# A planner's due times set anew in a gated-linear-attention and squared-ReLU kernel on one core

## The chip, the core and the metric

The kernel runs on one core of a Trainium2 chip. A core has five engines with a queue of instructions each: TensorE (PE, the matmuls; its weight loads are shown as PEld), VectorE (DVE), ScalarE (ACT), GpSimd (POOL) and SyncE (SP), which here issues all the DMAs. Every engine takes its own queue strictly in order; engines meet at semaphores only. The metric is the device time of one execution in microseconds. Three executions of the kernel before took 517.08, 519.09 and 520.18 us; the median is 519.09 us.

## The reference

```python
def _attn_ref(q, k, v, alpha):              # (4, 8, 768, 48) each
    state = np.zeros((B, H, D, D))
    for t in range(S):
        state = alpha[:, :, t, :, None] * state + np.einsum('bhd,bhe->bhde', k[:, :, t], v[:, :, t])
        y[:, :, t] = np.einsum('bhd,bhde->bhe', q[:, :, t], state)
    return y

def _moe_ref(x, w_in, w_out):               # (3072, 384), (384, 2048), (2048, 384)
    h = np.maximum(x @ w_in, 0.0)
    return h * h @ w_out
```

The attention's output, turned to (3072, 384), is the x of the second function. The weights arrive as float64, the rest as float32.

## The kernel before

**Blocks and groups.** The attention is computed in 24 blocks of 128 time steps (6 chunks of each of 4 batch entries; a block has all 8 heads). Two blocks make a pair, four blocks a group of 512 tokens: groups 0 to 5. While TensorE runs the feed-forward layers of group g, the attention of the two pairs of group g+1 is woven in between its matmuls. The first group's attention stands ahead of everything, in an order written out by hand (the string `first`, L980 to L989).

**Attention of a pair** (`attention`, L1018, with the step list `PLAN`, L996). Each step has an offset in units from the pair's start. `ln` (ACT) takes the logarithm of alpha; `sp` (DVE, L279, L280) splits it in two; `cs` (PE, L291, L292) sums it along time; `eb` and `ei` (ACT, L305, L310) make the decays; `mk` and `mq` (DVE, L314) scale k and q; `turn` (PE, L529) transposes them into four PSUM banks; `kc` and `qc` (ACT, L537) copy them out, eight copies for a pair. `ga` (L486) makes the scores and the state sums of the pair's first block in two banks (`sckv`) and begins the outputs y of the pair before in two more; `gb` (L509) ends y and does the scores and sums of the second block. Behind the scores DVE copies the masked part (`am`, L426), adds the state (`us`, L452, and `s`, L466) and multiplies it by the block's last decay row (`s`, L467). That row comes over DRAM: `bl` (SP, L327, `row<-b`) stores it, `br` (SP, L333, `last<-row`, two DMAs a block) loads it turned. Blocks 20 to 23 are the last chunk and need no state behind them. `ev` (L539, L562) copies y to x, twelve ACT copies for a pair, and frees the two banks.

**The feed-forward layers** (`layer_in`, L724, and `layer_out`, L884). From group 1 on the inputs and the weights are held as split values (a or b: the large part; l: the rest; d: a difference), so that a product takes three passes. The first layer has 16 h tiles of 128x512: `in_x(n)` is six matmuls, `in_y(n)`, two tiles later, three (L681). How an h tile is summed, put through ReLU and squared is told by a letter of a four-letter string, by n modulo 4 (`in_x`, `in_y`, `in_post`):

- D: ACT copies the tile out of PSUM (L696), DVE adds what `in_y` made (L594, which frees the bank), DVE does ReLU and square in one instruction (L710).
- A: ACT scales the tile in PSUM (L698), later takes ReLU out of PSUM (L715, which frees the bank) and squares (L719).
- M: as A, but DVE squares.

Then h is split as well: ACT makes the large part (L655), DVE the rest (L656) and the difference (L594). `split_h` keeps the parts in a ring of seven; `layer_out` puts split i no further ahead than seven tiles (`AHEAD + MORE`). In groups 2 to 4 the second layer is turned: `turned_x(n)` is six matmuls (L843), `turned_y` the d passes (L855). Groups 0 and 1 run part of the second layer as plain float32 (`out_plain`, L776, four PE instructions each), since the weights' parts are only just made there (`prepare`, L639: `cast_w` on ACT, `rest_w` and `diff_w` on DVE, and their stores).

**PSUM.** All eight banks are one pool: h tiles, `sckv`, y, T, cs and the sums of the second layer take them in turn.

**The streams.** The b parts stay in SBUF, the l and d parts are loaded again for each group from DRAM, 384 KB each (L648). `pump` (L644) issues the next load whenever a part was used up, as long as less than `room` parts are held; 16 of them are b parts, and the pool has 26 buffers.

**The planner.** `weave` (L1052) walks through the units of a group (`in_x` costs 1.05, `in_y` 0.53, `turned_x` 1.08, `out_plain` 1) and puts each event of the attention, of the weights' preparation and of the x splits (`splits_of_x`) ahead of the first unit that begins at or behind its due time. The due times are numbers in the table `AT` (L19): `g1` and `g` hold the starts of the pairs in group 1 and in groups 2 to 4, `ga` and `gb` their offsets, `gx` the x splits, `lead` the first h splits, `s0` and `ahead` how far the h splits run before the second layer, `w_first`, `w_in_at`, `w_in_by`, `wstep`, `o0`, `o2` the weights, `tp` and `tp1` the letters, `room1` and `room` the stream. Order matters only within an engine: what moves past work of other engines alone stands where it stood.

Of the kernel before, what the change touches and what calls it, by code (L numbers as in the profile page):

```python
# [15 lines left out]


GB = 4
AT = {'u0': 2, 'evs': 0.4, 'lead': 5, 'post': 3, 'w_first': (42.68, 45.29, 95.05), 'wstep': 2.32, 'w_in_at': 1.99, 'w_in_by': 3.14, 'room1': 24, 'room': 24, 's0': 1, 'ahead': 5, 'late': 23, 'xs': 0.22, 'g0': (-0.17, 20.59, 27.02), 'sc0': (2.36, 2.26, 2.42), 'g1': (4.41, 18.74, 27.21), 'g': (2.58, 19.59), 'g1x': 46.81, 'gx': 43.15, 'g0x': 55.58, 'k0': 2, 'h0': 20, 'k1': 5, 'h1': 0, 'h1by': 3, 'evs0': 0.13, 'tp': 'DAMD', 'tp1': 'AADD', 'split': 8, 'o0': (46.28, 49.2), 'o1': (), 'o2': (21.54, 19.65, 30.49, 25.39, 42.39, 50.96), 'str1': 13.05, 'ga': 10.14, 'gb': 12.14}  # L19


RUN = {0: 128, 32: 32, 64: 64, 96: 32}
# [3 lines left out]
def kernel(  # L26
# [243 lines left out]

    SPLIT = AT["split"]

# [314 lines left out]
    here, todo, room = {}, [], [22]  # L587
# [37 lines left out]
    def diff_w(w, p):  # L625
# [7 lines left out]
        for x in "ld":  # L633
            t = made.pop((x, w, p))
            if w == "i" or p >= NW - AT["k0"] or (x == "l" and p >= NW - AT["k1"]):
                here[x, w, p] = t
        pump()

    def prepare(at, w, p):  # L639
        step = AT["wstep"]  # L640
        fs = (cast_w, rest_w, diff_w)
        return [(at + i * step, f, (w, p)) for i, f in enumerate(fs)]
# [78 lines left out]
    def splits_of_x(at, g):  # L721
        return [(at + i * AT["xs"], f, (g, i % KM)) for i, f in enumerate((split_x,) * KM + (diff_x,) * KM)]

    def layer_in(g):  # L724
        units = []
        for n in range(NJ + 2):
            if n < NJ:
                units.append((1.05, in_x, (n,)))
            if 0 <= n - 2 < NJ:
                units.append((0.53, in_y, (n - 2,)))  # L730
            if 0 <= n - AT["post"] < NJ:
                units.append((0, in_post, (n - AT["post"],)))
            if AT["lead"] <= n < AT["lead"] + AHEAD and (g > 1 or AT["k1"] == NW):
# [240 lines left out]
    for x in "stky":  # L974
# [6 lines left out]
        zeros2 ln0 cs0 ln1 eb0 cs1 load0v ei0 mq0 mk0 load2a eb1 qT0 load3a qc0 mq1  # L981
        kT0 kc0 load1v ei1 qT1 mk1 load2k load2q qc1 sc0 kT1 weights0 kc1 kv0 load3q
        am0 lt1 sc1 ln2 us0 ln3 cs2 lt0 am1 load3k kv1 cs3 eb2 us1 ei2 gt1 mk2
        load2v ya0 weights1 yb0 lc1 gy0 eb3 kT2 mq2 load3v lc0 qT2 ei3 load4a zeros2
        st0 ea00 kc2 qc2 ed01 ed02 first0 zeros2 load4q mq3 zeros2 mk3 qT3 middle0
        qc3 kT3 second0 first1 kc3 lt3 lt2 sc2 kv2 am2 ea03 us2 sc3 kv3 gk3 middle1
        lc3 am3 us3 ha0 ya2 yb2 weights2 second1 weights3 ea20 lc2 ed21 ha1 ha3 ed22
        ed23 weights4 first2 st2 middle2 ha2 hb0 load4v hb1 st3 st1 load4k
    """  # L989
    for word in first.split():  # L990
        f = max((x for x in steps if word.startswith(x)), key=len)
# [167 lines left out]
```

## Time and profile before

| | us |
|---|---|
| median of three executions | 519.09 |
| lowest, highest | 517.08, 520.18 |
| the profiled execution, whole | 517.32 |
| its span in the profile | 515.3 |

Busy time of the engines by stage, from the view of windows of the profiled execution (the stages are cut where the groups' first `in_x` begins):

| stage | from, to (us) | PE | DVE | ACT |
|---|---|---|---|---|
| attention of group 0 and start | 0 to 30 | 27.76 | 19.25 | 17.98 |
| group 0 | 30 to 124.6 | 94.60 | 83.42 | 73.23 |
| group 1 | 124.6 to 212.65 | 87.18 | 74.88 | 59.92 |
| group 2 | 212.65 to 291.4 | 78.75 | 56.36 | 45.46 |
| group 3 | 291.4 to 371 | 78.69 | 52.68 | 45.45 |
| group 4 | 371 to 445.6 | 74.60 | 46.09 | 41.06 |
| group 5 and the end | 445.6 to 515.3 | 65.96 | 36.62 | 26.70 |

The span runs from the first instruction to the last; the 2 us between span and whole execution lie around it. A row of a group view gives line, engine, operation, out<-in, shape and count, then busy microseconds, mean nanoseconds of one, the idle time just before and what ended it. Consecutive instructions on DVE and ACT overlap a little, so that an instruction of 0.69 us takes some 0.6 us of the queue.

### The profile page before, as it was taken

What the parts mean: (1) busy time and instruction counts of PE and PEld (TensorE: products, weight loads), DVE (VectorE), ACT (ScalarE), POOL (GpSimd) and SP (SyncE); (2) the same over time, 40 slices, a digit from 0 to 9 for tenths busy, and PEclk for the clock granted to TensorE, in tenths of its full rate; (3) what the DMA queues carried; (4) which work ended last, traced back from release to release, by engine and by line L of the source; (5) the groups of instructions that cost most, each with busy time, mean ns of one, the idle gap of its engine ahead of it and who ended that gap; (6) DMA issues with size and microseconds to landing.
All of it is one profiled execution on the core that took longest, in us unless ns stands there. A gap on an engine that the chain in (4) does not pass through costs nothing.

```text
span 515.3 us, 12727 instructions
## 1 busy us (share of the span) xinstructions
PE 507.5 (99%) x5166; PEld 403.9 (78%) x5166; DVE 369.3 (72%) x640; ACT 309.8 (60%) x643; POOL 6.0 (1%) x33
## 2 busy tenths in 40 slices
PE   8999999999999999999999999999999999999997
PEld 6884456669887679988888887888888888888996
DVE  3798799879979868875886476685466486364861
ACT  4789875577879567386944174955175755164620
POOL 4000000000000000000000000000000000000000
PEclk9999999999999999999999999999999999999999
DMA  9989767153877886898876588966576534589301
GB/s 172 229 249 278 216 170 230 28 187 137 289 204 218 204 186 164 301 309 220 241 166 210 150 221 222 277 183 193 164 215 238 197 114 150 154 273 402 152 1 62
DMA packets 144795, 102.73 MB, mean 199 GB/s; under 512 B 116561, under 2 KB 118241, under 8 KB 144737
## 3 DMA queue, kind: packets, MB, share of 16 engines
q1 hardware_dynamic: 144736, 101.92, 69.0%
q8 instruction: 41, 0.67, 0.6%
q14 instruction: 18, 0.14, 0.1%
HBM read 84.57 MB, written 17.33 MB: 198 GB/s over the span
## 4 chain that ended last, share of the span: by engine, by line
PE 91%; DVE 4%; DMA 2%; SPq 1%; ACT 1%; issue 1%; DVEq 0%; POOLq 0%
PE h L681 29%; PE o L760 20%; PE o L843 13%; PE h L931 8%; PE o L855 6%; PE y L398 4%; PE sckv L418 2%; PE T L529 2%; PE sckv L441 2%; DMA last<-row 1%; PE cs L288 1%; DMA a_in<-in_alpha_dram 1%; PE zeros L384 1%; SPq L333 1%; DVE wl L618 1%; SPq L122 1%
## 5 line engine op out<-in xcount | busy, mean ns | idle before, releaser
L681 PE MATMUL h<-xa,wb 128*128 128x512 f32 x240 | 68.5, 393 | 0.9 <-DVE hid L594 0.9
L681 PE MATMUL h<-xl,wl 128*128 128x512 f32 x240 | 67.6, 390 | 0.0
L681 PE MATMUL h<-xd,wd 128*128 128x512 f32 x240 | 66.6, 392 | 0.0
L562 ACT COPY x<-y 32x256 f32<-32x256 f32 (+1 forms) x137 | 49.2, 365 | 25.3 <-PE y L398 23.1
L696 ACT ACTIVATE hid<-h 128x512 f32<-128x512 f32 x40 | 23.7, 600 | 61.2 <-PE h L681 61.2
L594 DVE TENSOR_TENSOR hid<-h,hid 128x512 f32<-128x512 f32 x40 | 27.6, 689 | 36.5 <-PE h L681 34.3
L681 PEld LDWEIGHTS h<-xl,wl 128*128 128x128 f32 x240 | 45.0, 188 | 9.7
L681 PEld LDWEIGHTS h<-xa,wb 128*128 128x128 f32 x240 | 44.4, 188 | 10.2 <-DVE hid L594 1.0
L681 PEld LDWEIGHTS h<-xd,wd 128*128 128x128 f32 x240 | 44.6, 188 | 9.3
L760 PE MATMUL o<-w_out,hid 128*128 128x384 f32 x144 | 48.9, 492 | 0.0
L931 PE MATMUL h<-x,w_in 128*128 128x512 f32 (+1 forms) x120 | 43.0, 511 | 0.0
L760 PEld LDWEIGHTS o<-w_out,hid 128*128 128x128 f32 x144 | 26.7, 190 | 17.2
L698 ACT ACTIVATE h<-h 128x512 f32<-128x512 f32 x40 | 23.3, 581 | 24.8 <-PE h L681 22.7
L655 ACT ACTIVATE ha<-hid 128x512 fp32r<-128x512 f32 x42 | 26.2, 637 | 15.9 <-DVE hl L656 11.4
L931 PEld LDWEIGHTS h<-x,w_in 128*128 128x128 f32 x120 | 22.4, 190 | 16.9 <-issue 13.4
L855 PE MATMUL o<-hd,wd 128*128 128x512 f32 x144 | 33.4, 391 | 0.0
L855 PEld LDWEIGHTS o<-hd,wd 128*128 128x128 f32 x144 | 26.8, 188 | 6.1 <-ACT o L848 0.6
L656 DVE SCALAR_TENSOR_TENSOR hl<-ha,hid 128x512 fp32r<-128x512 f32 x42 | 28.9, 687 | 3.5 <-ACT ha L655 3.5
L656 DVE SCALAR_TENSOR_TENSOR hx<-hx,hid 128x512 fp32r<-128x512 f32 x36 | 24.7, 686 | 9.1 <-ACT hx L655 9.1
L594 DVE TENSOR_TENSOR hd<-ha,hl 128x512 fp32r<-128x512 f32 x42 | 29.1, 692 | 1.7
L843 PE MATMUL o<-hx,wb 128*128 128x512 f32 x72 | 28.7, 399 | 0.0
L843 PE MATMUL o<-ha,wb 128*128 128x512 f32 x72 | 28.3, 393 | 0.0
(131 smaller groups left out, 987.5 us busy)
## 6 DMA issues: line engine op xcount, KB each, us to landing
wd<-do SPq DMA_DIRECT2D x37, 384.0 KB
wl<-lo SPq DMA_DIRECT2D x34, 384.0 KB
wl<-li SPq DMA_DIRECT2D x32, 384.0 KB
wd<-di SPq DMA_DIRECT2D x32, 384.0 KB
raw<-in_moe_w_in_dram SPq DMA_DIRECT2D x8, 768.0 KB
raw<-in_moe_w_out_dram SPq DMA_DIRECT2D x8, 768.0 KB
v_in<-in_v_dram SPq DMA_DIRECT2D x24, 192.0 KB
a_in<-in_alpha_dram SPq DMA_DIRECT2D x22, 192.0 KB
```

Of the source, the lines that this page charges most:

```text
L398: ins = nc.tensor.matmul(out=ys[e][64 * half : 64 * half + D + G * e, m % 2, p // 2, t], lhsT=lhsT, rhs=rhs, start=(half, e) not in seen, ...
L562: copy(out=x[kk][to : to + m, t : t + 2], in_=blk[n]["y"][e][r : r + m, :, p // 2],)
L594: nc.vector.tensor_tensor(out=o, in0=x, in1=z, op=op)
L655: nc.scalar.activation(out=a, in_=x, func=AF.Copy, scale=NEAR * E)
L656: nc.vector.scalar_tensor_tensor(out=l, in0=a.bitcast(FP32), scalar=-1.0 / E, in1=x, op0=ALU.mult, op1=ALU.add)
L681: nc.tensor.matmul(out=acc["h", j], lhsT=here[w, "i", p][:, kk, jj * 128 : (jj + 1) * 128], rhs=x_parts[x][:, kk], start=start and kk == 0 ...
L696: nc.scalar.activation(out=hid[j], in_=x, func=AF.Copy, scale=E)
L698: nc.scalar.activation(out=x, in_=x, func=AF.Copy, scale=1.0 + E)
L760: nc.tensor.matmul(out=acc[t][:, 0:DM], lhsT=lhs[:, t * C : (t + 1) * C], rhs=rhs, start=start, stop=stop, skip_group_check=True,)
L843: nc.tensor.matmul(out=acc[c], lhsT=by_parts(here[w, "o", p], jj, c), rhs=x, start=n == 0 and w == "b", stop=n == NJ - 1 and w == "l", ski ...
L855: nc.tensor.matmul(out=acc[c], lhsT=by_parts(here["d", "o", p], n % 2, c), rhs=h_diff[n], start=False, stop=last and n == NJ - 1, skip_gro ...
L931: nc.tensor.matmul(out=ps, lhsT=w[:, kk, c0 : c0 + 128], rhs=xT[g][kk][:, cols], start=(kk == 0), stop=(kk == KM - 1),)
```

## The change

No instruction is added or taken away but for one letter; what changes is the order in each engine's queue. In the table: the second pair of groups 2 to 4 begins 4.17 units earlier (19.59 to 15.42) and the first 0.28; the first pair of group 1 begins 3.27 units later. `ga` comes 0.82 units earlier in a pair, `gb` 0.83 later. The letters of groups 2 to 5 go from D A M D to D D A D. The h splits begin a tile earlier in the first layer, three of them instead of one stand ahead of the second layer, and they run up to 12 instead of 5 tiles ahead (the ring of seven still holds). The x splits of groups 2 to 4 begin 3.29 units earlier. The stream may hold 26 parts instead of 24 (25 in group 1). In groups 0 and 1 the preparation of a few weights and three h splits change places. In the order written out for the start, `mq2` goes ahead of `lc1`, and `lc0` and three loads of weights change places with work of other engines.

```diff
-AT = {'u0': 2, 'evs': 0.4, 'lead': 5, 'post': 3, 'w_first': (42.68, 45.29, 95.05), 'wstep': 2.32, 'w_in_at': 1.99, 'w_in_by': 3.14, 'room1': 24, 'room': 24, 's0': 1, 'ahead': 5, 'late': 23, 'xs': 0.22, 'g0': (-0.17, 20.59, 27.02), 'sc0': (2.36, 2.26, 2.42), 'g1': (4.41, 18.74, 27.21), 'g': (2.58, 19.59), 'g1x': 46.81, 'gx': 43.15, 'g0x': 55.58, 'k0': 2, 'h0': 20, 'k1': 5, 'h1': 0, 'h1by': 3, 'evs0': 0.13, 'tp': 'DAMD', 'tp1': 'AADD', 'split': 8, 'o0': (46.28, 49.2), 'o1': (), 'o2': (21.54, 19.65, 30.49, 25.39, 42.39, 50.96), 'str1': 13.05, 'ga': 10.14, 'gb': 12.14}
+AT = {'u0': 2, 'evs': 0.4, 'lead': 4, 'post': 3, 'w_first': (45.82, 44.44, 94.99), 'wstep': 2.31, 'w_in_at': 1.92, 'w_in_by': 3.02, 'room1': 25, 'room': 26, 's0': 3, 'ahead': 12, 'late': 23, 'xs': 0.35, 'g0': (-0.17, 20.59, 27.02), 'sc0': (2.36, 2.26, 2.42), 'g1': (7.68, 18.74, 27.21), 'g': (2.3, 15.42), 'g1x': 47.42, 'gx': 39.86, 'g0x': 55.51, 'k0': 2, 'h0': 16, 'k1': 5, 'h1': 0, 'h1by': 5, 'evs0': 0.23, 'tp': 'DDAD', 'tp1': 'AADD', 'split': 8, 'o0': (42.39, 46.35), 'o1': (), 'o2': (21.54, 19.65, 30.49, 26.1, 43.38, 50.96), 'str1': 14.0, 'ga': 9.32, 'gb': 12.97}
...
-        load2v ya0 weights1 yb0 lc1 gy0 eb3 kT2 mq2 load3v lc0 qT2 ei3 load4a zeros2
+        load2v weights1 ya0 mq2 yb0 lc1 gy0 eb3 kT2 lc0 load3v qT2 ei3 load4a zeros2
...
-        lc3 am3 us3 ha0 ya2 yb2 weights2 second1 weights3 ea20 lc2 ed21 ha1 ha3 ed22
-        ed23 weights4 first2 st2 middle2 ha2 hb0 load4v hb1 st3 st1 load4k
+        weights2 lc3 am3 us3 ha0 ya2 yb2 second1 weights3 ea20 lc2 ed21 ha1 ha3
+        weights4 ed22 ed23 first2 st2 middle2 ha2 hb0 load4v hb1 st3 st1 load4k
```

## The prediction

> **What bounds it now.** The page first: how much of the span has TensorE busy, and at what clock.
>
> ```profile
> span 515.3 us, 12727 instructions
> ...
> PE 507.5 (99%) x5166; PEld 403.9 (78%) x5166; DVE 369.3 (72%) x640; ACT 309.8 (60%) x643; POOL 6.0 (1%) x33
> ...
> PEclk9999999999999999999999999999999999999999
> ```
>
> A busy matmul may still be a stalled one, so the chain of waits is asked for its pitch:
>
> ```profile
> 280.44 10.96 PE o L855 x48
> ...
> 371.02 6.81 PE h L681 x30
> ```
>
> That is 0.228 and 0.227 us a matmul, and every long piece of L681 and L855 in the chain has this pitch. An in_x is thus 1.37 us, an in_y 0.68; the planner's unit is 1.3 us. The change adds no matmul, so the time can fall only by the waits that TensorE still has, and the view of waits, TensorE alone, lists them:
>
> ```profile
> PE warm L244 <- POOL s L67: 1.1, 1, 1.1
> PE h L681 <- DVE hid L594: 0.9, 1, 0.9
> PE cs L291 <- DVE us L452: 0.9, 1, 0.9
> PE cs L288 <- ACT a_in L267: 0.6, 1, 0.6
> PE sckv L418 <- DVE ks L371: 0.2, 1, 0.2
> ```
>
> First, fourth and fifth belong to the start, which keeps its order on PE. The second and third, 1.8 us, are all there is to win in the groups. The timelines tell where they are from. DVE in group 3:
>
> ```profile
> 312.83 0.36 DVE L466 TENSOR_TENSOR s<-sckv,us 128x192 f32<-128x192 f32 x1
> 316.78 0.36 DVE L467 TENSOR_TENSOR s<-s,last 128x192 f32<-128x192 f32 x1 [3.59 <-DMA last<-row]
> 317.05 0.68 DVE L594 TENSOR_TENSOR hid<-h,hid 128x512 f32<-128x512 f32 x1
> ```
>
> DVE stood 3.59 us for the last row of block 18; the add queued behind it frees a PSUM bank, and in_x(10), at 317.79, waited for that. The row is late since SP's queue was:
>
> ```profile
> 301.94 1.72 SPq L122 DMA_DIRECT2D a_in<-in_alpha_dram  x2
> 303.76 3.98 SPq L327 DMA_DIRECT2D row<-b  x1
> ...
> 310.87 4.38 SPq L333 DMA_DIRECT2D last<-row  x4
> ```
>
> The third wait, at 174.2, is DVE's backlog in group 1: scores of block 10 were masked at 173.05, 2.7 us behind their sums, and cs of block 12 wanted their bank.
>
> **The change, part by part.** I list each queue's order before and after by the due times, and count instructions by the durations of their rows (in the queue, 0.6 us for a DVE or ACT instruction of 0.69 or 0.6).
>
> *Group 1, third wait.* Ahead of the masks of block 10 DVE no longer has split 7 (0.69 + 0.69) and a rest_w (1.2): 2.6 us less. But the first pair's DVE work begins 3.27 units (4.3 us) later, and DVE waits for its first add at 9 us into the group, so that some of the relief goes. Counted through, the masks come 2.5 us behind the sums, much as before; but cs of block 12 now stands two units behind ga, not one: 1.29 us more. The 0.87 us goes but for 0 to 0.3; I take **-0.8**.
>
> *Group 3, second wait.* ga moves ahead of in_y(6), by 0.68 us, and gb behind in_x(10), so that 4.1 us of matmuls (in_y, in_x, in_y, in_x) stand between them where 2.05 stood. Should the row land at the same time, DVE waits 4.3 us, but in_y(6) is now an A tile, which needs no add, and TensorE next lacks a bank at in_x(11), about 318.5, with the add of tile 7 due at 318.3. 0.91 becomes 0 to 0.3: **-0.8**.
>
> *New waits, group 1.* At turn of blocks 8 and 9 mq(9) is behind an add, a rest_w and a diff_w more than before: it ends 20.0 us into the group, and is wanted at 19.9 without stall (0.5 at most if each DVE instruction costs 5% more). Queued behind it on DVE is the preparation of parts 5 and 6, for which only ACT and stores wait. **+0.3**. At turn of blocks 12 and 13 gb stands two units ahead, not three. The twelve ACT copies that free y's banks take 4.36 us; they began 1.8 us behind gb before, since a cast_w was ahead of them, and can begin at 0.8 now. They end 5.2 us behind gb's start, and turn's second half wants the banks at 4.7 to 4.8: **+0.4** (0 to 0.5). Behind it on TensorE is all else.
>
> *Groups 2 and 3, second pair.* Between cs and turn there are now 4.1 us of matmuls (in_y, in_x twice) instead of 5.5. ACT's queue from one to the other end of in_x(10) to cs: two ln (0.8), ReLU and square of tile 6 (1.15), the scaling of tile 10 (0.55), twelve copies (4.6), two copies of D tiles (1.0): 8.1 us in 6.7 us, so eb begins 1.4 us behind cs. Then eb, ei, eb, ei at 0.39 each, and DVE: mk, a square, mq, mk, mq, 0.5 to 0.6 each. mq(21) ends 4.9 us behind the start of cs and turn wants it 5.5 behind: 0.6 us to spare. **0**, with up to 1.4 us a group if ACT comes later. turn to ga: 3.4 us of matmuls, eight ACT copies (2.3 us) end 1.5 us ahead: 0. In group 4 the second pair has no new blocks.
>
> *Group 2, last rows of block 16.* DVE is ready for it 7.5 us behind turn's start (1.15 + 3.4 + scores and sums 1.1 + masks and adds 1.8). In the same pair before, turn was at 254.05 and the last SP issue of the rows ended at 258.6; with 2 us to land (the 1.9 of the chain's `last<-row`) that is 6.5 us. 1 us to spare: **0**, at worst, if the 3.98 us hold of group 3 comes here, DVE is 3 us late, split 3 with it, and turned_x(3) waits 1.6.
>
> ```profile
> 246.21 1.27 SPq L122 DMA_DIRECT2D a_in<-in_alpha_dram  x2
> ...
> 249.35 0.26 SPq L327 DMA_DIRECT2D row<-b  x1
> ```
>
> These packets are the one place where a page speaks against the change. The Trainium skill, "DMA: Bandwidth & Descriptors", Specifications, has line rate only from 512 B a transfer; the page of the profile counts 116,561 of 144,795 packets below that, the alpha loads' among them. By that rule every `row<-b` behind two alpha loads would be held, and the moved pair would pay the 1.6 us; the trace shows 3.98 us in one place and 0.26 here, so the loads alone don't do it.
>
> *M to D.* Four tiles a group leave ACT a scaling and a ReLU (581 + 596 ns) and take a copy (600); DVE gets an add (689) beside the square (686). ACT -2.3 us, DVE +2.8 us a group. DVE is busy 52.7 of 79.6 us in group 3: hidden, **0**; without that cover 2.8 us a group. The add frees a bank a unit sooner than the ReLU did.
>
> *h splits.* DVE needs 1.22 us for each (hl, hd), TensorE 1.37 for each turned_x, and the splits start as early as before or earlier: 0. Past ring place 7 ACT waits for the turned_x before; queued there are copies of y, which nothing wants for 15 us. *x splits*: wanted 10 us later, 0. *Group 0*: TensorE's order is untouched, the four weight parts and the h splits trade places within 25 us in which DVE has gaps of 3 us in all; 0 (-0.3 to 0.3). *The start*: only mq2 passes lc1 on DVE, 0.16 us, and qT2 waits for neither: 0.
>
> *Room.* A load now goes into the buffer just used, so SP follows TensorE instead of running two parts ahead of the frees; the parts land two uses sooner. No wait of the trace is on a streamed part: 0 in this execution. In the others, which took up to 2.9 us more, I can't see what they waited for; late rows and parts are the likeliest, and both are eased.
>
> **Sum**: -0.8 - 0.8 + 0.3 + 0.4 = -0.9; the profiled 517.32 (a span of 515.3 and 2.0 around it, which stays) becomes 516.4. The median of the runs before is 1.8 us above the profiled one; if all of that stays, the median is 518.2, if none, 516.4. I let a tenth to a fifth stay: **516.6**.
>
> **The rivals.** *B, no new wait*: the turns fit, and both waits go: 517.32 - 1.8 = 515.5, with the start's small change 515.3. For it: the margins that I find negative are 0.1 and 0.4 us. *C, given back*: the waits reappear elsewhere as PSUM stays as full (y's banks are held 1.65 units longer); or half the diff is without effect, as `ahead` over 7 and the moved weight loads are: 519. *D, slower*: the second pair, moved into the first layer, doesn't fit. Its place is turn at 22 units of groups 2 and 3, its price 1.4 us each for ACT's backlog plus 1.6 us for block 16's row: 517.32 - 0.9 + 4.4 = 520.8, with the median's 1.8 us 522.6. It decides once ACT is 0.6 us later at cs than I count. For it: ACT is busy 9.56 of 10 us from 240 to 250 before. Against: D tiles relieve ACT just there.
>
> **Chances.** Forecast 0.45 (its own range 515.0 to 518.3), B 0.18, C 0.14, D 0.23. A measurement of this kernel tells about 0.5% from no change: below 516.5 is faster, above 521.7 slower. Forecast gives 0.25 faster and 0.20 same; B faster; C same; D 0.22 slower, 0.01 same. Faster 0.43, same 0.35, slower 0.22. Range 513.8 (below B by a start or end that shrinks) to 522.6.
>
> **What would show it.** In the profile after: no wait of in_x on L594 near 317 and none of cs on `us` in group 1; turns of group 1 late by 0.3 to 0.4 us; turn of the second pair in groups 2 and 3 without a wait on DVE q_in. ACT falls by some 9 us, DVE grows by 11. A wait at these turns above 1 us, or of L467 on `last<-row` in group 2, proves D; PE waits of the same sum at other lines prove C.

## The result and the profile after

| | before | after |
|---|---|---|
| median of 13 executions, us | 518.25 | 516.34 |
| lowest, highest | 517.08, 520.18 | 515.71, 517.53 |
| the profiled execution, whole | 517.32 | 516.64 |
| its span | 515.3 | 514.6 |

The ratio is 0.9964, with a 95% interval of 0.9953 to 0.9975: 1.9 us are gone in the median, and only 0.7 us in the two executions that were profiled. That difference is what most of the experiments are about. The page of the kernel after, its first lines and its chain:

```profile
span 514.6 us, 12773 instructions
...
PE 508.3 (99%) x5166; PEld 404.6 (79%) x5166; DVE 377.0 (73%) x656; ACT 302.3 (59%) x627; POOL 6.0 (1%) x33
...
PE 96%; DMA 2%; SPq 1%; DVE 1%; issue 0%; ACT 0%; DVEq 0%; POOLq 0%
```

ACT has lost 7.5 us and DVE gained 7.7, as the letters want it. The view of waits for TensorE in the kernel after:

```profile
PE warm L244 <- POOL s L67: 1.1, 1, 1.1
PE cs L288 <- ACT a_in L267: 0.5, 1, 0.5
PE sckv L418 <- DVE hid L594: 0.2, 1, 0.2
PE sckv L418 <- DVE ks L371: 0.2, 1, 0.2
```

Both waits of 0.9 us in the groups have gone, and one new wait has come: `sckv` on L594. From each group's first in_x to the next one's, before and after (the differences of the starts in the timeline):

| stage | before | after | difference |
|---|---|---|---|
| start and group 0 | 124.43 | 124.36 | -0.07 |
| group 1 | 88.06 | 87.75 | -0.31 |
| group 2 | 78.75 | 79.42 | +0.67 |
| group 3 | 79.62 | 78.65 | -0.97 |
| group 4, group 5 and the end | 144.40 | 144.39 | 0 |

Group 3 shows how its wait went. DVE and then PE in the timeline of the kernel after:

```profile
317.05 0.36 DVE L467 TENSOR_TENSOR s<-s,last 128x192 f32<-128x192 f32 x1 [4.24 <-DMA last<-row]
317.33 0.68 DVE L710 SCALAR_TENSOR_TENSOR hid<-hid 128x512 f32<-128x512 f32 x1
317.93 0.68 DVE L594 TENSOR_TENSOR hid<-h,hid 128x512 f32<-128x512 f32 x1
```

```profile
317.90 0.66 PE L441 MATMUL sckv<-v_in,k_in 64*64 64x48 f32 x32
318.49 0.97 PE L681 MATMUL h<-xd,wd 128*128 128x512 f32 x3
319.30 0.85 PE L681 MATMUL h<-xa,wb 128*128 128x512 f32 x3
```

DVE stands longer than before (4.24 us, 3.59 then), and TensorE no longer notices, since the add that it wants comes after more of its own matmuls. In group 2 the same lateness is now felt. DVE and PE there:

```profile
237.04 0.36 DVE L467 TENSOR_TENSOR s<-s,last 128x192 f32<-128x192 f32 x1 [3.61 <-DMA last<-row]
237.31 0.68 DVE L710 SCALAR_TENSOR_TENSOR hid<-hid 128x512 f32<-128x512 f32 x1
237.92 0.69 DVE L594 TENSOR_TENSOR hid<-h,hid 128x512 f32<-128x512 f32 x1
```

```profile
238.14 0.28 PE L418 MATMUL sckv<-qs,ks 48*64 48x64 f32 x2
238.66 0.63 PE L418 MATMUL sckv<-qs,ks 48*64 48x64 f32 x27 [0.24 <-DVE hid L594]
```

Here `gb`'s second bank is the one that the add of 237.92 frees, and TensorE stands from 238.20 to 238.66.

### The profile page after: what moved, and what is told of

Read it like the earlier page. It is cut to its first block, busy times and chain, and to the rows that moved or that the text cites. A ratio compares the mean times of both kernels' runs of the same rounds, so it can differ in the third digit from the quotient of the medians.

```text
span 514.6 us, 12773 instructions
## 1 busy us (share of the span) xinstructions
PE 508.3 (99%) x5166; PEld 404.6 (79%) x5166; DVE 377.0 (73%) x656; ACT 302.3 (59%) x627; POOL 6.0 (1%) x33
## 4 chain that ended last, share of the span: by engine, by line
PE 96%; DMA 2%; SPq 1%; DVE 1%; issue 0%; ACT 0%; DVEq 0%; POOLq 0%
PE h L681 31%; PE o L760 22%; PE o L843 13%; PE h L931 8%; PE o L855 6%; PE y L398 4%; PE sckv L418 3%; PE T L529 2%; PE sckv L441 2%; PE cs L288 1%; DMA a_in<-in_alpha_dram 1%; PE zeros L384 1%; DMA last<-row 1%; PE cs L291 1%; SPq L333 1%; PE cs L292 1%
## 5 line engine op out<-in xcount | busy, mean ns | idle before, releaser
L696 ACT ACTIVATE hid<-h 128x512 f32<-128x512 f32 x56 | 33.7, 601 | 88.4 <-PE h L681 86.7
L681 PE MATMUL h<-xd,wd 128*128 128x512 f32 x240 | 68.4, 398 | 0.0
L594 DVE TENSOR_TENSOR hid<-h,hid 128x512 f32<-128x512 f32 x56 | 38.5, 689 | 33.9 <-PE h L681 33.6
L710 DVE SCALAR_TENSOR_TENSOR hid<-hid 128x512 f32<-128x512 f32 x56 | 37.8, 684 | 0.0
L594 DVE TENSOR_TENSOR hd<-ha,hl 128x512 fp32r<-128x512 f32 x42 | 29.1, 692 | 1.9
L843 PE MATMUL o<-hx,wl 128*128 128x512 f32 x72 | 28.0, 389 | 0.0
```

Of the source, the lines that this page charges most:

```text
L594: nc.vector.tensor_tensor(out=o, in0=x, in1=z, op=op)
L681: nc.tensor.matmul(out=acc["h", j], lhsT=here[w, "i", p][:, kk, jj * 128 : (jj + 1) * 128], rhs=x_parts[x][:, kk], start=start and kk == 0 ...
L696: nc.scalar.activation(out=hid[j], in_=x, func=AF.Copy, scale=E)
L710: nc.vector.scalar_tensor_tensor(out=h, in0=h, scalar=0.0, in1=h, op0=ALU.max, op1=ALU.mult)
L843: nc.tensor.matmul(out=acc[c], lhsT=by_parts(here[w, "o", p], jj, c), rhs=x, start=n == 0 and w == "b", stop=n == NJ - 1 and w == "l", ski ...
```

## The experiments

All are compared with the kernel before, run beside them on the same chip (its medians there were 517.67 to 518.47). The kernel after was not run beside them. A difference to it is one of medians taken at different times, between which the kernel before alone moves by 0.8 us; where it is small, the difference by the two ratios to the kernel before is given as well. The first four each take one part of the change alone.

**e1_pairs**

```diff
- 'g': (2.58, 19.59), 'gx': 43.15, 'ga': 10.14, 'gb': 12.14
+ 'g': (2.3, 15.42), 'gx': 39.86, 'ga': 9.32, 'gb': 12.97
```

> The kernel before with four due times of the kernel after alone: g, ga, gb and gx, that is the pairs of groups 2 to 4, their scores and the x splits. Theory (DVE's wait for the late last decay row is what the kernel before loses in groups 2 and 3, more in other executions than in the profiled one, and the wider distance of ga and gb takes it up): most of the 1.9 us, median 1.0 to 1.6 below the kernel before; TensorE's wait of in_x on L594 in group 3 is gone. Rival 'stream': at most 0.5 below. Rival 'letters' (without the D tiles ACT is too late for the second pair): slower than before by 0.5 to 2.8, with a wait at the second pair's turn.

Measured: 519.13 us, ratio 1.0014 (1.0000 to 1.0029). Groups 2 and 3 took 78.81 and 78.63 us, so the wait on L594 is gone as the theory has it, and turn waits for nothing. But group 1 took 90.51, 2.45 more than before. The view of waits for PE, and PE's timeline there:

```profile
PE y L398 <- issue: 1.5, 2, 1.1
...
PE sckv L441 <- issue: 1.2, 1, 1.2
```

```profile
179.07 0.32 PE L441 MATMUL sckv<-v_in,k_in 64*64 64x48 f32 x8
180.63 0.56 PE L441 MATMUL sckv<-v_in,k_in 64*64 64x48 f32 x24 [1.24 <-issue]
```

TensorE stops in the middle of one loop of equal matmuls, for "issue", that is for nothing that the profile knows. No theory of mine had that. The view of DMA has a queue of kind "instruction", 41 packets of 16 KB. I numbered TensorE's records (matmuls, weight loads, waits) from the start of the program, and looked where such stops lie: every one follows record 192 of a run of 256 (counted from 0), and ends 1.3 to 1.6 us behind the landing of one of these 41 packets. From the records:

```
kernel      place us  packet landed  TensorE goes on  later by
e1_pairs    169.63    169.66         170.95           1.29
e1_pairs    179.17    179.16         180.63           1.47
e2          16.96     17.12          18.52            1.40
e2          317.90    317.33         318.72           1.39
after       169.93    168.87         170.29           1.42
```

So TensorE waits for its own instructions. 256 of them are 29 us of large matmuls (0.227 us for a matmul and its weight load) and under 2 us of the scores (0.45 us for 32 and 32). A packet that comes late costs nothing in the first case and its whole lateness in the second. This became the new theory, "supply".

**e2_first_groups**: `g1`, `g1x`, `g0x`, `w_first`, `wstep`, `w_in_at`, `w_in_by`, `o0`, `o2`, `h0`, `h1by`, `str1` of the kernel after in the kernel before.

> The kernel before with the due times of groups 0 and 1 of the kernel after alone: g1, g1x, g0x, the w_ entries, o0, o2, h0, h1by, str1. Theory: only the wait of cs on us in group 1 is at stake, 0.9 us in the profiled execution; ga and gb keep their old offsets, so that the masks of block 10 come as late as before and cs of block 12 stands one unit behind ga: 0 to 0.6 below the kernel before. Rival 'first groups' (the median's gain is from group 1, where weights and pairs compete for DVE): 1.2 to 1.9 below.

Measured: 519.94 us, 1.0039 (1.0021 to 1.0057); the executions spread from 518.2 to 522.9. Group 1 took 87.94 us, and cs waits for `us` no more; both theories fall on the total. The profiled execution lost 1.56 us at 16.96 and 0.82 at 317.90, both places of the table above, and both in stretches that this edit leaves alone. What makes the packets land later there in this kernel was not found.

**e3_letters**

```diff
- 'tp': 'DAMD'
+ 'tp': 'DDAD'
```

> The kernel before with the letters D D A D in place of D A M D alone (four tiles a group copied by ACT, added and squared by VectorE). Theory: hidden work moved from ACT to DVE, 0, within 0.4 of the kernel before; DVE longer by some 7.7 us of busy time, ACT shorter by 7.5. Rival 'VectorE is what the row wait delays, and more work on it makes it worse': 0.5 to 1.5 above. Rival 'ACT frees banks late, the letters carry the gain': 1 to 1.9 below.

Measured: 517.90 us, 0.9998 (0.9988 to 1.0008): the letters alone are worth nothing in the median, as the prediction had it. In the profiled execution one wait changes. DVE stands 3.44 us for the row of block 18, and `ga` and `gb` are where they were, but the built program gives in_x(10) of group 3 the bank of tile 6 in place of that of tile 7, and it waits 0.23 us on L715 instead of 0.9 on L594. Stops for instructions (1.14 us in all, below) hide that in the total.

**e4_room**

```diff
- 'room1': 24, 'room': 24
+ 'room1': 25, 'room': 26
```

> The kernel before with the stream's room alone (26 parts held instead of 24, 25 in group 1). Theory: no wait is on a streamed part; SP's order changes around the last rows: 0, within 0.5 of the kernel before. Rival 'stream' (the other executions of the kernel before wait for parts or for rows behind a pump that runs ahead): 1 to 1.9 below.

Measured: 521.69 us, 1.0067 (1.0054 to 1.0079). Both theories are wrong. The orders of PE, DVE, ACT and POOL are those of the kernel before, only SP's differs. The view of waits for PE, and three windows:

```profile
PE h L681 <- ACT x L562: 2.5, 1, 2.5
```

```profile
319.00:323.00 4.00, 1.50 (x7) 0.94 (x6) 2.86 (x6) 3.17 (x9) 0.00 (x0) 1.00 1.08 295
323.10:326.40 3.30, 3.30 (x9) 2.53 (x9) 0.00 (x0) 1.01 (x3) 0.00 (x0) 0.50 0.44 88
326.50:330.00 3.50, 3.50 (x17) 2.86 (x17) 0.77 (x2) 1.85 (x4) 0.00 (x0) 1.00 0.71 227
```

(After the window and its length come the busy times of PE, weight loads, DVE, ACT and POOL, then TensorE's granted clock, the DMA share and GB/s.) in_x(11) of group 3 waits 2.5 us for the copies of y. Which bank a tile gets is fixed when the program is built: in the kernel before this tile has the bank of an h tile 15 tiles back, here that of `y` five tiles back, which `gb` has only just finished. Another order of loads was enough to change the choice. And the wait costs more than itself: behind it the granted clock stands at 0.50 for 3.4 us, which is 1.7 us more. 2.5 + 1.7 is most of the 4.3 us by which group 3 is longer (83.95); besides, in_x(10) has the bank of tile 6 here too and waits 0.4 us on L715 in place of the 0.9 on L594.

The next four take the kernel after and put one thing into it, or one part back.

**e5_shift**

```diff
+        for i in range(28 if _ == 2 else 0):
+            e, p = i % 2, i // 2 % NP
+            rows = slice(64 * e, 64 * e + 64)
+            nc.tensor.matmul(
+                out=t[rows, p, G:64], lhsT=s_t[0][rows, p, :], rhs=s_t[0][rows, p, G:64],
+                start=True, stop=True, skip_group_check=True,
+            )
...
-        warm(0)
+        warm(_)
```

> The kernel after with 28 small matmuls on zeros (112 instructions of TensorE) added to the warm-up at the start; nothing behind them changes. Theory 'supply': TensorE's instructions arrive by DMA in packets of 256 (the DMA view shows 41 of 16 KB); in every trace so far each stall put down to issue in the scores lies 192 instructions past a multiple of 256 and ends 1.4 us behind the landing of such a packet. In the kernel after only few of these places lie in or right behind a burst of small matmuls. 112 instructions more put three of them there, near 233, 257 and 312 us: 2.7 to 5.1 us above the kernel after, 519.0 to 521.5, with waits of 0.5 to 2 us for issue at these three places. Rival 'the place does not matter' (the stalls are a matter of DMA load alone): only what the added matmuls take at the start, at most 1 us: 516.3 to 517.4.

Measured: 528.77 us in the median of five executions, ratio 1.0188 to the kernel before (1.0154 to 1.0223), 12.4 us above the kernel after. Nothing behind the start was touched, the banks neither. The stops came at 237.48 (1.59 us), 262.35 (1.89; TensorE goes on 1.36 us behind a landing there too, though the profile names DVE) and 319.79 (3.23). PE's timeline (line numbers are 8 higher here), and the DMA view of the 1.6 us in which the packet for the third landed:

```profile
319.35 0.66 PE L406 MATMUL y<-am,v_in 64*48 64x64 f32 x27
323.03 0.33 PE L406 MATMUL y<-am,v_in 64*48 64x64 f32 x4 [3.02 <-issue]
```

```profile
DMA packets 1325, 0.17 MB, mean 104 GB/s; under 512 B 1324, under 2 KB 1324, under 8 KB 1324
...
q8 instruction: 1, 0.02, 5.6%
```

The places were told in advance within 8 us (233, 257 and 312), and they came later by about what the start and the earlier stops had added; the rival is out. The size was not: a fourth stop of 2.04 us fell at 16.50, and behind it and behind the one of 3.23 the clock was halved for 3.41 us each. Groups by parts: the start and group 0 are 4.8 us longer, group 2 is 2.7, group 3 is 4.9. The packet landed among 1,324 small data packets.

**e6_old_distance**

```diff
- 'ga': 9.32, 'gb': 12.97
+ 'ga': 10.14, 'gb': 12.14
```

> The kernel after with ga and gb at the offsets of the kernel before (10.14 and 12.14). Theory (the distance of 4.1 us of matmuls between the two bursts of scores is what takes up the late row and the instruction supply): the wait of in_x on L594 in group 3 is back, and 0.8 to 2.0 us above the kernel after, 517.1 to 518.3. Rival 'letters and room carry it': within 0.4 of the kernel after.

Measured: 525.02 us, 1.0143 (1.0125 to 1.0161), far above what was expected. The view of waits for PE:

```profile
PE h L681 <- ACT x L562: 2.4, 1, 2.4
PE T L529 <- DVE k_in L314: 2.4, 1, 2.4
...
PE h L681 <- ACT hid L715: 0.5, 1, 0.5
PE h L681 <- DVE hid L594: 0.3, 1, 0.3
```

The wait on L594 in group 3 is not back: in_x(10) has been given the bank of tile 6, an A tile, and waits 0.5 us on L715; the 0.3 on L594 is in group 2 (242.67). The large waits are others: turn in group 1 waits for its scaled k, and in group 3 in_x(11) has got the bank of y five tiles back once more, as in e4_room. Behind each of the two the clock is at half for 3.4 us. The wide distance is thus needed by the rest of the table as it is built; the expected sum was wrong since it priced one wait, and neither the bank nor the late k.

**e7_old_letters**

```diff
- 'tp': 'DDAD'
+ 'tp': 'DAMD'
```

> The kernel after with the letters D A M D of the kernel before. Theory: ACT has 0.5 to 0.6 us more to do between cs and turn of the second pair, and my count left 0.6 us to spare: 0 to 0.5 us above the kernel after, 516.3 to 516.9, no wait of turn above 0.3. Rival D of the prediction (the second pair fits only if ACT is relieved): 1.4 to 2.8 above, with T waiting for q_in at the second turn of groups 2 and 3.

Measured: 516.76 us, 0.9981 (0.9970 to 0.9992); 0.4 above the kernel after by the medians, 0.9 by the ratios, and no turn waits. Rival D of the prediction falls.

**e8_old_room**

```diff
- 'room1': 25, 'room': 26
+ 'room1': 24, 'room': 24
```

> The kernel after with 24 parts of the stream held, as before. In the kernel before, 26 instead of 24 cost 3.5 us, since the built program then gave in_x of group 3 the bank of y. Theory: room itself is worth nothing, and only the banks that come with it count; here two h tiles swap the banks of an h tile and of y, far behind y's copies: within 0.5 of the kernel after. Rival 'room is worth 3.5 us the other way here' or 'the stream needs it': 1 us or more above the kernel after.

Measured: 516.89 us, 0.9987 (0.9977 to 0.9997); 0.55 above the kernel after by the medians, 1.2 by the ratios. The profiled execution has one stop more, 0.59 us at 390.61 in group 4, a place of the supply. It stands in the two other wide-distance kernels with 24 parts as well (0.61 in e1_pairs, 0.61 in e11) and in none with 26 parts. A stop of that size, from SP's order around one packet of instructions, would be most of the 0.55; that it is the whole of what room is worth here is not shown. In e4_room the same step cost 3.5 us the other way, by a bank.

Two experiments then went for the late rows. Both exchange the loads of a pair's two rows: DVE wants the first block's first, and the plan issues it second.

**e9_rows_first**, in the kernel after, and **e10_rows_first_before**, in the kernel before:

```diff
-        (6.5, "turn br1"),
-        (7.0, "kc0 qc0 kc1 qc1 br0"),
+        (6.5, "turn br0"),
+        (7.0, "kc0 qc0 kc1 qc1 br1"),
```

> The kernel after with the two loads of last<-row of a pair exchanged: the pair's first block, whose row DVE wants first, is issued first (br0 with turn, br1 half a unit later). All banks stay as they are. Theory: in group 2 DVE stands 3.61 us at L467 for the row of block 14, and the add behind it holds up gb by 0.45 us; the row's two issues come 1.0 us earlier, DVE stands some 2.6 us, and 0.3 to 0.5 us go: 515.8 to 516.1. Rival 'backlog' (all four small loads land together when the queue is drained): DVE still stands 3.4 us or more, within 0.2 of the kernel after.

> The kernel before with the same exchange of the two loads of rows, banks unchanged. Theory: DVE's 3.59 us at L467 in group 3 become some 2.6, in_x(10) finds its bank, and the second wait of the prediction goes: 0.8 to 1.0 us below the kernel before. If late rows are also what the other executions of the kernel before lose, 1.3 to 1.9 below; if it is the instruction supply, no more than 1.0. Rival 'backlog': nothing, within 0.3.

Measured: e9 516.21 us, 0.9957 (0.9945 to 0.9968); e10 518.31, 0.9994 (0.9984 to 1.0005). The waits came as the theory said. DVE in group 2 of e9, and in group 3 of e10:

```profile
236.63 0.36 DVE L467 TENSOR_TENSOR s<-s,last 128x192 f32<-128x192 f32 x1 [2.58 <-DMA last<-row]
```

```profile
317.06 0.36 DVE L467 TENSOR_TENSOR s<-s,last 128x192 f32<-128x192 f32 x1 [2.91 <-DMA last<-row]
```

In e9 group 2 takes 78.87 us where it took 79.42, and `gb` waits no more; in the median 0.13 us of it can be seen, within the intervals. In e10 in_x(10) waits no more and group 3 is 0.6 us shorter; the median falls by 0.16 us, within an interval of -0.8 to +0.3.

That the exchange did this is not shown, since rows come as early without it. In e8_old_room the rows are loaded in the old order, and TensorE's order and the banks of group 2 are those of the kernel after:

```profile
236.10 0.36 DVE L467 TENSOR_TENSOR s<-s,last 128x192 f32<-128x192 f32 x1 [2.60 <-DMA last<-row]
```

In e7_old_letters DVE stands 2.33 us there, and in neither does `gb` wait. In group 3 DVE stands 3.74 us in e9 and 3.17 in e7; it stands 2.91 in e10, and 3.44 and 3.26 in e3 and e4. So the lateness of a row differs between executions by as much as the exchange was to bring, and the wait of `gb` is one that some executions have. The profiled execution of e10 has four stops at places of the supply, 1.37 us in all.

**e11_pairs_and_first_groups**: the edits of e1_pairs and e2_first_groups together, in the kernel before.

> The kernel before with the due times of both e1_pairs and e2_first_groups (ga, gb, g, gx, g1 and the weights), old letters, room, splits and start. Alone they cost 0.9 and 1.8 us. Theory: together they bring ga of group 1 away from the places where TensorE stood for its instructions (169.6 and 179.2 in e1_pairs), and all but the letters' 0.4 and the room's 0.5 is there: 516.7 to 517.6, groups 1 to 3 within 0.5 us of the kernel after. Rival 'each costs what it costs alone': 520 to 521.

Measured: 517.16 us, 0.9972 (0.9962 to 0.9982). Two parts that cost 0.9 and 1.8 us alone gain 1.3 together; group 1 takes 87.67 us, and of the stops of e1_pairs there only one of 0.25 us is left.

**e12_second_pair_back**

```diff
- 'g': (2.3, 15.42), 'gx': 39.86
+ 'g': (2.58, 19.59), 'gx': 43.15
```

> The kernel after with the pairs of groups 2 to 4 and their x splits back at the places of the kernel before (g 2.58 and 19.59, gx 43.15), ga and gb wide as after. Theory: the move of the second pair is worth nothing of its own (the prediction's 0 for it); the wide distance keeps the places where instructions run out away from the scores of the second pair too (264 and 344 us, where the kernel before has 0.3 us at times): within 0.6 of the kernel after, 515.8 to 516.9. Rival 'the second pair had to leave the second layer': 1 us or more above the kernel after, 517.3 or more, with a wait at the second pair of groups 2 and 3.

Measured: 516.30 us, 0.9976 (0.9960 to 0.9992). By the medians that is the kernel after, by the ratios 0.6 us more, and the intervals overlap: no gain from bringing the second pair forward by itself can be told.

**Where the median's gain is from.** The stops at places of the supply (idle time beyond the usual pitch), summed over one profiled execution each:

```
TensorE's order of before:   before 0.08   e3 1.14   e4 0.79   e10 1.37   (the last three: mean 1.10)
TensorE's order of after:    after 0.44    e7 0.29   e9 0.82   e8 1.32   e11 1.01   (mean 0.78)
```

In e8 and e11, which hold 24 parts, 0.57 and 0.59 us of this is the stop near 390; without it the five make a mean of 0.54. The profiled execution of the kernel before was a lucky one: of the 13 others one is shorter. Six places have a packet landing less than 1.9 us ahead of need in its order (near 16, 28, 193, 265, 316 and 345 us), and three have in the order after (17, 28, 170). The distance of `ga` and `gb`, 4.1 us of matmuls for 2.05, puts more large matmuls into every run of 256 that reaches over both; e6, which takes nothing but the distance back, has six such places again (near 16, 28, 196, 241, 266 and 320). The executions add up: e10's profiled 517.69 us is the 517.32 of before, with 1.37 - 0.08 of stops more and the wait of 0.91 less. Its kin lose some 1.0 us more than the profiled execution of before, which is about the 0.93 us by which the median stood above it; that the executions behind this median lose it in the same way is likely, but they were not traced. In the order after, the median stands 0.3 below the profiled execution; what these 0.3 are stays open (the start's wait for `a_in` alone goes from 0.2 to 1.4 us over all the profiles). So of the 1.9 us the 0.7 of the profiled pair are shown. By an estimate from these sums another 0.3 to 0.6 are stops for instructions that are rarer now (1.10 for the kin alone, 0.84 with the kernel before itself, against 0.54). The rest, 0.6 to 0.9, was not traced. The samples are four and five executions.

No run is clearly faster than the kernel after; e9's 516.21 and e12's 516.30 lie within the intervals.

## Why the prediction was right, and where it was not

The number (516.6) and the direction held, the reason for the median not. The sum held by most of its terms, and in total partly by luck: groups 1 and 3, counted at -0.9, brought -1.28, and group 2, counted at 0, took 0.67 of it back.

- *Group 1, third wait (-0.8) and the new waits at the turns (+0.3, +0.4).* Right in kind. The wait of cs is gone. The third quarter of the turn of blocks 8 and 9 and that of blocks 12 and 13 come 0.2 us late each; y's twelve copies end at 182.20, and the turn goes on at 182.25, where the count had them end at 182.3. Net -0.31 where -0.1 was predicted, with a stop of 0.36 for instructions that was not foreseen.
- *Group 3, second wait (-0.8).* Right: -0.97, and DVE's own wait of 4.24 us against a predicted 4.3. in_x(11) wants the bank of tile 7, as told, and finds it. One reason given is none: tile 6 needed no add as an M tile either. What takes in_x(10) off the late add is the bank that the build gives it: that of tile 7 in the kernel before, one of `sckv` in the kernel after and in e1, that of tile 6 in e3 and e4.
- *Groups 2 and 3, second pair (0, and rival D).* Right: turn does not wait, e7 shows it doesn't hang on the letters either, and e12 shows no gain from the move.
- *Group 2, last rows of block 16 (0).* Right for that block. A hold of SP's queue, which the prediction drew from the 512 B of the Trainium skill's "DMA: Bandwidth & Descriptors", Specifications, did come to the moved pair (2.01 us at 245.42, 0.26 before), and the microsecond to spare covered it: L467 follows at 256.41 without a wait. What holds the queue is not shown. What failed is the step beside it: it looked at the moved pair alone. The first pair's row, block 14's, came late, and `gb` had been given the bank of a D tile whose add stands behind L467: that is 0.46 of the +0.67 us of group 2 in the profiled execution. It is a term left out, of the size of those counted, which e7, e8 and e9 do not pay in theirs.
- *M to D (0).* Right alone in the median (e3); 0.4 to 0.9 in the company of the rest (e7). ACT -7.5 and DVE +7.7 us, counted as -9 and +11.
- *Room (0, and ease for the other executions).* Right here by luck: to hold more parts costs nothing in the kernel after (24 take 0.55 to 1.2 us more, e8) and 3.5 us in the kernel before (e4). That a different order of loads changes banks was in no step.
- *The median.* "A tenth to a fifth stays" was near, since none stayed, but the offset of 1.8 us was one of three executions; over thirteen it is 0.93. So the 0.3 us between forecast and measurement owe something to luck. The reason given, late rows and parts, is not borne out: no profile has TensorE waiting for a part, and e10's median hardly moves with the wait for the row gone from its profile. What the runs show in its place is the supply of instructions: about 1.0 us in the three kin of the kernel before.

## What to carry to other kernels

Read a stall for "issue" inside a burst of small matmuls as TensorE waiting for its own program, and number the instructions: a burst of 256 or more in 2 us is at the mercy of one DMA packet, and moving anything ahead of it, even dead work, moves the place. Break such bursts with large matmuls between. When parts of a table are tried one by one, look at what else each changes (banks fixed at the build, these places): here two losses made a gain, and a gain in one table was a loss in the other.

## What was not expected of the hardware

- TensorE goes on 1.3 to 1.7 us behind the landing of a 16 KB packet of its instructions, in all stops of 0.25 us or more of the fourteen traces; where the landing was more than that ahead of need, no stop is in the trace.
- A TensorE wait of 2.4 us or more is followed by 3.4 us at a granted clock of 0.50 (e4_room, e5_shift, e6_old_distance), so that 2.5 us cost 4.2; stops of 1.3 and 1.5 us in e1_pairs and of 1.6 and 1.9 in e5_shift left the clock at full. The stop of 2.04 us at the start of e5_shift, amid small matmuls, was followed by it too. The Trainium skill, "TensorE: Matmul & The Clock Gate", Part 1, has the clock fall to half after one idle window of about 3.4 us; the length of the slow stretch agrees with the trace, while for the idle time 2.5 us were enough here (1.50 us busy of the 4.00 in the window above).
- Which of two tiles waits for y's copies was decided by SP's order of loads, through the choice of banks at the build: 2.5 us in e4_room.
